# Reordering the split products of a packed matrix step: plain halves, whole products, special halves

## The chip, the cores and the metric

The kernel runs on one core of one Trainium2 chip. The metric is the device time of one execution in microseconds (us). Before the change it is 2581.51 us, the median of three runs that lie between 2581.0 and 2581.97 us.

TensorE is the matrix engine; the profile shows it as two rows, PE for the matmuls and PEld for the loads of the stationary operand (the weights). DVE, ACT and POOL are the vector, scalar and GpSimd engines, SP is the queue that issues most of the DMAs.

## What is computed

The reference filters a sequence in the frequency domain and sends the result through a small network:

```python
X = np.fft.rfft(x, axis=1)              # x: (8, 3008, 256)
Y = X * (filt_r + 1j * filt_i)[None]
y = np.fft.irfft(Y, n=3008, axis=1)
h = y.reshape(8 * 3008, 256) @ w_in     # (256, 2048)
out = (h - np.tanh(h)) @ w_out          # (2048, 256)
```

Everything is float32.

## The kernel before

The length 3008 is taken as 64 times 47. A transform over the 64 (`first`) is followed by a *middle stage* (`middle`): a transform over the 47, the product with the filter, and the transform back over the 47. A last transform over the 64 (`last`) gives the tokens, and the network follows: `up` (by `w_in`), `shrink` (h minus tanh h) and `down` (by `w_out`).

The eight batch elements are cut into 48 groups, and each group into four units of the network. The network keeps TensorE busy all the time; the transforms of later batch elements are spread between its units. A loop over the units (line 1280) calls `up`, and at fixed places in it the callback `t(k)` (line 1325) takes one step of whatever stage is due: `first`, `last`, or a step of `middle`. Everything is issued in program order, written out by hand; no planner moves an instruction. So the order of the Python calls is the order on each engine.

`middle(b)` runs for seven batch elements (b = 1 to 7; element 0 goes another way). It goes over four slices `o = 0..3`. Each slice has

- a *forward* step (lines 433 to 443): `packed` writes four PSUM banks (`t`, `o3`, `o1`, `o2`) from the tile `a2`. ACT copies banks 2 and 3 (line 438), DVE adds and subtracts (lines 440 and 441);
- the product with the filter, on DVE (lines 445 to 461);
- a *backward* step (lines 462 to 469): `packed` writes four banks (`o0`, `t`, `y`, `o1`) from the tile `xy`; ACT and DVE copy them out (line 465), and DMAs take them to memory.

The bank names other than `t` are shared with the network: `o0` to `o3` are the accumulators of `down`, `y` is a bank of `up`. After a forward step TensorE goes on with `down` (line 747), after a backward step with `down` or `up` (lines 747 and 577).

`packed` (line 346) makes 16 small products at once. Each product has 24 rows by 32 columns of weights and sits in its own square of the 128 by 128 array: row strip `q` (0 to 3, partitions 32q up) and column strip `col` (0 to 3). Row strip q writes bank q; column strip col writes the partitions 32 col and up of that bank. A *whole* product streams 512 columns of data: two blocks of 256 that use the same weights.

In the last slice, `o = 3`, one block of four of the products is special and needs other weights. These four products are *split*: a *plain half* (256 columns, usual weights) and a *special half* (256 columns, other weights), both in the same square of the array, the second writing the other half of the bank's columns. In the forward step these are the four products of column strip 3, one in each row strip. In the backward step they are the four products of row strip 3. So a split step has 12 whole products, 4 plain halves and 4 special halves, 20 in all; a *plain* step (o = 0, 1, 2) has 16 whole products.

A float32 product is carried out in two passes over the data: the profile shows two weight loads and two matmuls for every product. A split step thus has 40 matmul records, a plain step 32.

Before the change the plain half stands at its place in the order of q and col (in the forward step the 4th, 8th, 12th and 16th product, in the backward step the 13th to 16th), and the four special halves come behind all of them.

Of the kernel before, what the change touches and what calls it, by code (L numbers as in the profile page):

```python
# [17 lines left out]
BATCH, SEQ, DM = 8, 3008, 256  # L18
# [93 lines left out]
def kernel(  # L112
# [9 lines left out]
    nc = tc.nc  # L122
# [97 lines left out]
    def sums(u):  # L220

        w = (wu if u < 4 else wd)[:, :, 256 * (u % 4):256 * (u % 4) + 256]
        V.tensor_add(w[:, 4], w[:, 6], w[:, 3])
        yield
        for to, one_in, less in ((5, 4, 0), (2, 1, 5), (6, 0, 6)):
            V.tensor_sub(w[:, to], w[:, one_in], w[:, less])  # L226
            yield

    def begun(tiles, job, queue=nc.sync):
        j = converted(tiles, *job, queue)  # L230
        next(j)
        return j
# [3 lines left out]
    def weights(tiles, jobs, queue, began, ahead, after=()):  # L236

        began += [begun(tiles, job, queue) for job in jobs[len(began):ahead]]
        yield
        for k in range(len(jobs)):  # L240
            pending[0] = len(jobs) - k
            for n, _ in enumerate(began[k]):
                yield
                if after and n == 2 and k + 1 < len(jobs):
                    next(began[k + 1])
            if k + ahead < len(jobs):
                began.append(begun(tiles, jobs[k + ahead], queue))
            pending[0] = len(jobs) - k - 1
            for u in dict(after).get(k, ()):
                yield from sums(u)  # L250
# [94 lines left out]

    def packed(banks, o, weight, data):

        late = []
        for q, bank in enumerate(banks):
            part = slice(PAD * q, PAD * q + NH)  # L350
            for col in range(4):
                to, at = bank[PAD * col:PAD * col + PAD], data(q, col)[part]
                plain, special = (wide[part, weight(q, col, last)] for last in (0, 1))
                if o == 3 and 3 == (col if weight is WAYS[0] else q):
                    late.append((to[:, 1], special, at[:, DM:2 * DM]))
                    to, at = to[:, 0], at[:, 0:DM]
                else:
                    to = to.rearrange("p n c -> p (n c)")
                nc.tensor.matmul(to, plain, at, start=True, stop=True)  # L359
        for to, special, at in late:  # L360
            nc.tensor.matmul(to, special, at, start=True, stop=True)  # L361

    def forth(g, at, z):

# [62 lines left out]
    def middle(b, z):  # L427
# [4 lines left out]
        for o in range(4):  # L432
            there = z(("t", "o3", "o1", "o2"))
            packed(there, o, WAYS[0],
                   lambda q, col: a2[:, 2 * col:2 * col + 2].rearrange("p n c -> p (n c)"))
            there = [bank.rearrange("p n c -> p (n c)") for bank in there]
# [24 lines left out]
            yield  # L461
            again = z(("o0", "t", "y", "o1"))
            packed(again, o, WAYS[1], lambda q, col: xy[:, (0, 2, 1, 3)[col]])
            for j, copy in enumerate((ACT.copy, V.tensor_copy) * 2):
                copy(nn[:, 2 * j:2 * j + 2], again[j])
# [483 lines left out]
    with tc.tile_pool(name="tr", bufs=2) as tr, tc.manual_schedule():  # L949
# [16 lines left out]
        with tc.tile_pool(name="pro", bufs=1) as pro, \  # L966
# [112 lines left out]
            for c in range(3):  # L1079
# [7 lines left out]
                for k in (0, 4):  # L1087
                    nc.sync.dma_start(xt[0:64, k:k + 4], dram(x.tensor, (8 * c + k) * DM,
                                                              [[NR * DM, 64], [1, 4 * DM]]))
                    at = max(k, lo)  # L1090
# [77 lines left out]
            for g in range(last_g + 1):  # L1168
# [25 lines left out]
                if g == 2:  # L1194
                    next(turning)
                    ahead = [begun(tiles1, job, queue=G) for job in jobs[5:7]]
# [6 lines left out]
            late = weights(tiles1, jobs[5:], G, ahead, 3,  # L1203
                           after={6: (0,), 8: (1,), 10: (2, 4)})
# [5 lines left out]
        with tc.tile_pool(name="dn", bufs=2) as dn, \  # L1210
# [58 lines left out]
            for _ in range(4):  # L1269
                nc.tensor.matmul(warm[0:KM], mats[:, 3 * KM:4 * KM], mats[:, 3 * KM:3 * KM + 256],  # L1270
                                 start=True, stop=True)
# [8 lines left out]
            for U in range(total + 2):  # L1280
                i, u = divmod(U, 4)
                if U == 6:
                    assert not pending
                    late = (None for u in (3, 5, 6, 7) for _ in sums(u))
                if U == 3:
                    G.dma_start(mats[:, 0:10 * PAD], wide_d[0:KM])
                if U < total:
                    p, c = groups[i]
# [119 lines left out]
```

## Time and profile before

| what | value |
|---|---|
| time, median of three runs | 2581.51 us (2581.0 to 2581.97) |
| span of the profiled execution, first to last instruction | 2578.0 us |
| what the median has beside that span | 3.5 us; the profiled execution's own time is not listed apart from its span |
| PE busy | 2553.1 us, 99% of the span |
| DVE, ACT, POOL busy | 71%, 64%, 57% of the span |
| matmuls of `packed`, line 359 | 2 x 896 records, 33.4 us busy forward, 31.7 us backward |
| matmuls of the special halves, line 361 | 2 x 56 records, 7.2 us busy each way |

How to read it: the engines' busy times overlap, so the engine that is busy nearly all of the span and waits for nobody sets the time. Matmul records overlap one another too: a record lasts from the first column that goes in to the last result that comes out, so in a full stream a new matmul begins long before the record of the one ahead ends. What a matmul costs is therefore read from the distance between two starts, not from its duration. In the list in order of time, matmuls of one line that follow one another are merged into one row: start, length, engine, line, operation, tiles, shape, count. Starts and lengths there are in us.

### The profile page before, as it was taken

How to read it: one execution, taken by the hardware profiler on the slowest of the kernel's cores; microseconds unless marked ns; L12 is line 12 of the kernel's file. 1: busy time of each engine (PE TensorE's matmuls, PEld its weight loads, DVE VectorE, ACT ScalarE, POOL GpSimd, SP SyncE). 2: the span in 40 equal slices, each digit the busy share in tenths (PEclk: the TensorE clock that was granted, in tenths of full speed). 3: DMA queues.
4: the chain of work that ended last, by engine and by line, in shares of the span. 5: the costliest groups of instructions: out<-in, count | busy, mean ns of one | idle time of the engine just before them, and what ended most of it. 6: DMA issues, size and time to landing. Idle time of an engine off the chain costs nothing.

```text
span 2578.0 us, 43442 instructions
## 1 busy us (share of the span) xinstructions
PE 2553.1 (99%) x16596; PEld 2173.1 (84%) x16596; DVE 1818.7 (71%) x2235; ACT 1661.7 (64%) x2482; POOL 1465.8 (57%) x1124
## 2 busy tenths in 40 slices
PE   8999999999999999999999999999999999999998
PEld 7678889888898888988888888888889888898887
DVE  6888776777567775778657876588766877555555
ACT  4566666666666666666666666666666666666665
POOL 4356665666556655565646565566655766555552
PEclk9999999999999999999999999999999999999999
DMA  8863225332333324343243332334231322110110
GB/s 223 278 176 102 64 48 124 99 98 59 82 82 97 99 48 90 85 102 82 58 95 89 92 85 52 87 97 112 64 72 35 93 65 49 28 32 18 25 22 18
DMA packets 345334, 214.30 MB, mean 83 GB/s; under 512 B 245338, under 2 KB 316536, under 8 KB 341470
## 3 DMA queue, kind: packets, MB, share of 16 engines
q1 hardware_dynamic: 321551, 170.82, 28.1%
q10 hardware_dynamic: 12142, 23.60, 2.9%
q0 software_dynamic: 11424, 17.03, 2.4%
q8 instruction: 132, 2.16, 0.4%
q14 instruction: 85, 0.69, 0.1%
HBM read 130.72 MB, written 83.39 MB: 83 GB/s over the span
## 4 chain that ended last, share of the span: by engine, by line
PE 94%; DVE 2%; DMA 2%; ACT 1%; issue 1%; POOL 0%; ACTq 0%; SPq 0%; POOLq 0%; DVEq 0%
PE o L747 43%; PE x L577 25%; PE z L577 12%; PE y L577 6%; PE pm L359 2%; PE pu L536 2%; PE pf L306 1%; DMA ct<-a 1%; DMA x<-in_x_dram 0%; DMA ct<-e 0%; PE pm L361 0%; PE pf L294 0%; DVE h L699 0%; PE o L802 0%; DVE wd L226 0%
## 5 line engine op out<-in xcount | busy, mean ns | idle before, releaser
L747 PE MATMUL o<-t,wd 128*128 128x256 f32 (+1 forms) x3008 | 762.1, 376 | 0.0
L557 POOL TENSOR_TENSOR t<-h 128x512 f32<-128x512 f32 (+1 forms) x186 | 305.8, 1644 | 733.6 <-DVE h L699 713.7
L699 DVE TENSOR_TENSOR h<-h,y 128x1024 f32<-128x1024 f32 (+1 forms) x384 | 573.5, 1493 | 166.5 <-ACT y L695 163.0
L747 PEld LDWEIGHTS o<-t,wd 128*128 128x128 f32 x3008 | 569.2, 190 | 82.4 <-POOL o L775 15.1
L577 PE MATMUL x<-tu,wu 128*128 128x256 f32 (+1 forms) x2256 | 579.0, 379 | 0.0
L747 PE MATMUL o<-h,wd 128*128 128x256 f32 (+1 forms) x2256 | 572.8, 376 | 1.7 <-DVE h L699 1.7
L583 ACT COPY s<-x 128x512 f32<-128x512 f32 (+1 forms) x188 | 108.8, 579 | 595.8 <-PE x L577 554.1
L747 PEld LDWEIGHTS o<-h,wd 128*128 128x128 f32 x2256 | 426.0, 190 | 71.4 <-issue 20.5
L577 PEld LDWEIGHTS x<-tu,wu 128*128 128x128 f32 x2256 | 420.9, 190 | 66.8 <-issue 13.5
L692 ACT ACTIVATE y<-y 128x1024 f32<-128x1024 f32 (+1 forms) x384 | 399.2, 1040 | 12.1
L695 ACT ACTIVATE y<-y 128x1024 f32<-128x1024 f32 (+1 forms) x384 | 399.8, 1041 | 4.6
L689 ACT ACTIVATE y<-h 128x1024 f32<-128x1024 f32 (+1 forms) x384 | 400.3, 1043 | 3.5 <-DVE h L625 1.7
L558 POOL TENSOR_TENSOR t<-h,t 128x512 f32<-128x512 f32 (+1 forms) x186 | 305.4, 1642 | 14.6
L560 POOL TENSOR_TENSOR t<-h,t 128x512 f32<-128x512 f32 (+1 forms) x186 | 288.2, 1549 | 0.0
L559 POOL TENSOR_TENSOR t<-h 128x512 f32<-128x512 f32 (+1 forms) x186 | 287.5, 1546 | 0.0
L583 ACT COPY u<-x 128x512 f32<-128x512 f32 (+1 forms) x376 | 213.7, 568 | 56.3 <-PE x L577 53.6
L625 DVE COPY h<-x 128x512 f32<-128x512 f32 (+1 forms) x188 | 127.9, 680 | 135.0 <-PE x L577 134.7
L577 PE MATMUL y<-ut,wu 128*128 128x256 f32 (+1 forms) x752 | 190.1, 375 | 0.6 <-ACT a L296 0.6
L577 PE MATMUL x<-ut,wu 128*128 128x256 f32 (+1 forms) x752 | 190.1, 375 | 0.6 <-DVE h L625 0.6
L577 PE MATMUL z<-ut,wu 128*128 128x256 f32 (+1 forms) x752 | 190.2, 375 | 0.4 <-DVE h L617 0.4
L577 PE MATMUL z<-tu,wu 128*128 128x256 f32 (+1 forms) x752 | 190.1, 375 | 0.4 <-DVE h L633 0.4
L600 DVE TENSOR_TENSOR h<-y,s 128x512 f32<-128x512 f32 (+1 forms) x188 | 126.6, 673 | 68.5 <-PE y L577 61.9
(194 smaller groups left out, 2743.1 us busy)
## 6 DMA issues: line engine op xcount, KB each, us to landing
ft<-filt SPq DMA_DIRECT2D x28, 1024.0 KB
ct<-nn SPq DMA_DIRECT2D x56, 512.0 KB
e<-ct SPq DMA_DIRECT2D x47, 512.0 KB
a<-ct SPq DMA_DIRECT2D x112, 192.0 KB
out_dram<-ot SPq DMA_DIRECT2D x1248, 16.0 KB
x_sb<-in_x_dram SPq DMA_DIRECT2D x74, 256.0 KB
ct<-a ACTq DMA_DIRECT2D x62, 256.0 KB
gt<-g_pairs SPq DMA_DIRECT2D x42, 128.0 KB
```

Of the source, the lines that this page charges most:

```text
L557: by.tensor_sub(t[0], b[0][1], b[0][0])
L558: by.tensor_sub(t[1], b[1][1], t[0])
L559: by.tensor_sub(t[2], b[1][1], b[0][1])
L560: by.tensor_sub(t[3], b[1][0], t[1])
L577: nc.tensor.matmul(bank[:, k], wu[:, q - 1, (2 * u + k) * 128:(2 * u + k + 1) * 128], rhs[q - 1], start=(first and k == 0), stop=True, ski ...
L583: ACT.copy(t, X)
L625: V.tensor_copy(h[:, 2, :, 0:w], X)
L689: ACT.activation(y[k], ht[k], AF.Arctan, scale=TURN)
L692: ACT.activation(y[k], y[k], AF.Tanh, scale=BEND)
L695: ACT.activation(y[k], y[k], AF.Square, scale=SCALE, accum_out=y_sums[:, 2 * U + k // 2:2 * U + k // 2 + 1])
L699: V.tensor_mul(ht[k], ht[k], y[k])
L747: nc.tensor.matmul(product(q), wd[:, q - 1, (2 * u + k) * 128: (2 * u + k + 1) * 128], rhs[q - 1][:, k], start=(u == 0 and k == 0 and q == ...
```

## The change

In a split step `packed` collects its products in three lists and issues first the four plain halves, then the twelve whole products, then the four special halves. Plain steps issue the same 16 products in the same order as before. No product, weight or operand is changed, and the orders on DVE, ACT, POOL and SP are the same, instruction for instruction; only TensorE's order is another in the 14 split steps (7 forward, 7 backward). The new text is one line shorter, so that line 747 of before is line 746 after, and all matmuls of `packed` stand in line 360.

```diff
     def packed(banks, o, weight, data):
 
-        late = []
+        ahead, whole, late = [], [], []
         for q, bank in enumerate(banks):
             part = slice(PAD * q, PAD * q + NH)
             for col in range(4):
                 to, at = bank[PAD * col:PAD * col + PAD], data(q, col)[part]
                 plain, special = (wide[part, weight(q, col, last)] for last in (0, 1))
                 if o == 3 and 3 == (col if weight is WAYS[0] else q):
+                    ahead.append((to[:, 0], plain, at[:, 0:DM]))
                     late.append((to[:, 1], special, at[:, DM:2 * DM]))
-                    to, at = to[:, 0], at[:, 0:DM]
                 else:
-                    to = to.rearrange("p n c -> p (n c)")
-                nc.tensor.matmul(to, plain, at, start=True, stop=True)
-        for to, special, at in late:
-            nc.tensor.matmul(to, special, at, start=True, stop=True)
+                    whole.append((to.rearrange("p n c -> p (n c)"), plain, at))
+        for to, weights_of, at in ahead + whole + late:
+            nc.tensor.matmul(to, weights_of, at, start=True, stop=True)
```

On TensorE's list of instructions a forward split step turns from four times (three whole, one plain half), then four special halves into 4 plain halves, 12 whole, 4 special halves. The waits move with it: before, each row strip's first product waits for its bank and its rows of data, so that the waits stand at the 1st, 5th, 9th and 13th product. After, the four plain halves touch all four banks, and these waits stand at the 1st to 4th product. In six of the seven forward split steps (not in that of b = 1) the wait of the third row strip, bank `o1`, is among others for TensorE's own earlier matmuls; before it stands at the 9th product, after at the 3rd. In the backward step the wait for TensorE stays with the third row strip's first whole product (bank `y`), which is the 9th product before and the 13th after.

## The prediction

> **What bounds the kernel now.** I read the page first (busy time, clock, chain), then the waits of TensorE, then the list in order of time around the split steps.
>
> ```profile
> span 2578.0 us, 43442 instructions
> ...
> PE 2553.1 (99%) x16596; PEld 2173.1 (84%) x16596; DVE 1818.7 (71%) x2235; ACT 1661.7 (64%) x2482; POOL 1465.8 (57%) x1124
> ...
> PEclk9999999999999999999999999999999999999999
> ...
> PE 94%; DVE 2%; DMA 2%; ACT 1%; issue 1%; POOL 0%; ACTq 0%; SPq 0%; POOLq 0%; DVEq 0%
> ```
> ```profile
> PE pe L1049 <- POOL nn L397: 5.8, 3, 4.0
> PE o L747 <- DVE h L699: 1.7, 2, 1.6
> ```
>
> TensorE is the bound: it is busy 99% of the span at full clock and carries 94% of the chain that ended last. The two longest of its waits on other engines are 5.8 and 1.7 us in all, the first of them in the opening stage (line 1049), where no split step lies. So a microsecond taken off TensorE's stream between two middle steps should come off the time.
>
> The steps themselves: a plain backward and a split backward step, a plain forward and a split forward one, each with the matmul behind it.
>
> ```profile
> 2130.98 1.14 PE L359 MATMUL pm<-xy,mats_sb 24*32 24x512 f32 x32
> 2132.05 0.70 PE L747 MATMUL o<-t,wd 128*128 128x256 f32 x2
> ```
> ```profile
> 2183.74 1.11 PE L359 MATMUL pm<-xy,mats_sb 24*32 24x512 f32 x32
> 2184.37 1.08 PE L361 MATMUL pm<-xy,mats_sb 24*32 24x256 f32 x8
> 2185.39 0.48 PE L747 MATMUL o<-t,wd 128*128 128x256 f32 x1
> ```
> ```profile
> 2083.45 1.22 PE L359 MATMUL pm<-a,mats_sb 24*32 24x512 f32 x32
> 2084.60 0.70 PE L747 MATMUL o<-h,wd 128*128 128x256 f32 x2
> ```
> ```profile
> 2135.70 1.21 PE L359 MATMUL pm<-a,mats_sb 24*32 24x512 f32 x32
> 2136.34 1.08 PE L361 MATMUL pm<-a,mats_sb 24*32 24x256 f32 x8
> 2137.36 0.48 PE L747 MATMUL o<-h,wd 128*128 128x256 f32 x1
> ```
>
> From the first product to the next stage's first matmul a plain backward step takes 2132.05 - 2130.98 = 1.07 us, a plain forward step 1.15, a split step 1.65 in both directions. Both kinds stream the same number of columns through each square, so the split costs 0.58 us backward and 0.50 forward. All 14 are alike: the windows below show the first and the last of 14, each with 40 matmuls, and the mean.
>
> ```profile
> 327.90:329.60 1.70, 1.67 (x40) 0.60 (x40) 0.00 (x0) 0.00 (x0) 1.00 0.97 242
> ...
> 2183.70:2185.40 1.70, 1.66 (x40) 0.60 (x40) 0.44 (x1) 0.54 (x2) 1.00 0.00 0
> sum 23.80, PE 23.56 PEld 8.53 DVE 3.42 ACT 4.08; mean PE 1.68 PEld 0.61 DVE 0.24 ACT 0.29
> ```
>
> **Where the 0.58 us go.** Inside the backward step, by narrow stretches of the list (a merged row starts at its first record), and the durations in ns (least/median/most):
>
> ```profile
> 2184.06 0.79 PE L359 MATMUL pm<-xy,mats_sb 24*32 24x256 f32 x16
> 2184.19 0.66 PE L359 MATMUL pm<-xy,mats_sb 24*32 24x512 f32 x12
> 2184.80 0.41 PE L361 MATMUL pm<-xy,mats_sb 24*32 24x256 f32 x2
> 2185.05 0.41 PE L361 MATMUL pm<-xy,mats_sb 24*32 24x256 f32 x3
> ```
> ```profile
> L359 PE MATMUL pm<-xy,mats_sb x22: 374/612/612, 2183.7 to 2184.2; 24*32 24x512 f32 x14, 24*32 24x256 f32 x8
> L359 PE MATMUL pm<-xy,mats_sb x12: 587/587/587, 2184.2 to 2184.3; 24*32 24x512 f32 x12
> L361 PE MATMUL pm<-xy,mats_sb x8: 371/374/396, 2184.4 to 2185.1; 24*32 24x256 f32 x8
> ```
> ```profile
> 2184.81 0.17 PEld L361 LDWEIGHTS pm<-xy,mats_sb 24*32 24x32 f32 x6 [0.33 <-issue]
> ```
>
> The second passes of the plain halves start at 2184.06, those of the whole products at 2184.19, which is 0.45 us behind the first pass of the first product. A first pass of 256 columns, its weight load with it, holds its square 0.24 us (2184.81 to 2185.05); for a second, whose weights lie ready, I estimate 0.22 from that, so the squares of the halves are free from about 2184.28. Yet only one pass of a special half starts near there, at 2184.37; its second starts at 2184.80, and the other three special halves only then, their second passes at 2185.05. These times match the ends of the first product: its first pass ends at 2183.74 + 0.61 = 2184.35, its second at 2184.19 + 0.59 = 2184.78, and 0.02 us behind each comes a pass of the first special half. Forward it is the same, with the halves elsewhere in the order:
>
> ```profile
> 2136.16 0.76 PE L359 MATMUL pm<-a,mats_sb 24*32 24x512 f32 x12
> 2136.77 0.37 PE L361 MATMUL pm<-a,mats_sb 24*32 24x256 f32 x1
> ```
>
> 2135.70 + 0.61 = 2136.31 against 2136.34, and 2136.16 + 0.59 = 2136.75 against 2136.77. I read: the 17th product enters, pass by pass, only as the 1st completes; a later one waits behind it in order. TensorE holds 16 products at a time. The Trainium skill, "TensorE: Matmul & The Clock Gate", in its opening table, gives TensorE's queue a depth of 64; at two loads and two matmuls a product that is 16 products. By that page the place in the queue counts, not the kind of product ahead, and the time would be that of the sum below; without it the traces leave this open, which is rival two.
>
> **The change part by part.** Removed and added: nothing; 40 passes before and after, the other engines' orders untouched. Moved: the first product becomes a plain half. Times from here run from a step's first product.
>
> *Backward, seven steps.* Plain half 1: first pass 0, second pass 0.24 (the special halves show 2184.81 to 2185.05), its square free at 0.24 + 0.22 = 0.46. It completes at 0.40 and 0.24 + 0.37 = 0.61. Whole products start within 0.1 behind the halves and their second passes end as in a plain step, which then leaves at 1.07. Special half 1: first pass at 0.46 (square), second at 0.68 (square; the queue lets it in at 0.61 + 0.03 = 0.64). Special halves 2 to 4 come in order behind that entry: 0.65, 0.67, 0.68, spaced as in 2184.80 and its followers; the last one's second pass starts at 0.68 + 0.24 = 0.92. From that start to the next matmul it takes 0.30 now (2185.05 + 0.41 - 0.37 = 2185.09 to 2185.39). So the step ends at 1.22, 0.43 less than 1.65.
>
> *Forward, b = 1, one step.* Nothing waits inside; the same 1.22.
>
> *Forward, six steps.* Their third bank waits for TensorE's own earlier matmuls. The plain forward step shows the price: 1.15 against 1.07, so its 9th product starts 0.08 late, at 0.05 + 0.08 = 0.13. That wait now stands at the 3rd product: half 3 starts at 0.13, its second pass at 0.13 + 0.22 = 0.35, complete at 0.35 + 0.37 = 0.72, so that special half 4, behind the entry of special half 3's second pass, comes in at 0.75, with its second pass at 0.99 and the end at 1.29 or 1.30. All 12 whole products now stand behind this wait, not 8: they would leave at about 1.19, which is covered. Saved 1.65 - 1.30 = 0.35.
>
> *Cover and followers.* Nothing may take the gain back behind the step:
>
> ```profile
> 2137.45 1.07 ACT L438 COPY xy<-pm 128x512 f32<-128x512 f32 x2 [1.91 <-PE pm L361]
> ...
> 2183.49 0.73 POOL L775 TENSOR_TENSOR o<-pu,o 128x256 f32<-128x256 f32 x1 [1.97 <-DVE pu L773]
> ...
> 2184.86 1.07 ACT L465 COPY nn<-pm 128x512 f32<-128x512 f32 x2 [1.98 <-PE pm L359]
> ```
>
> ACT stands idle ahead of the copies, 1.91 us forward and 1.98 us backward; forward, they start some 0.4 us earlier, and the four DVE operations (lines 440 and 441) with them. Backward bank 0 is written 0.03 us later, four starts behind the halves, and ACT's first copy moves by that; were ACT's idle time gone, this would be what it costs. POOL was idle 1.97 us before 2183.49, so `t`, which line 747 reads behind the step, is long done; and plain steps reach the same followers at 1.07 with no wait. SP and POOL queues see no change; the output DMAs follow the copies.
>
> Sum: 8 x 0.43 + 6 x 0.35 = 3.4 + 2.1 = 5.5 us. The profiled span would become 2578.0 - 5.5 = 2572.5; the median stands 3.5 us above the span, so the time is 2581.5 - 5.5 = **2576.0 us**, -0.21%. Bounds of the unknown entry: at best split steps become plain ones (rival one, 7.4 us), at worst nothing is gained and the earlier wait is paid (rival two, -1 us). I take 5.5 because four coincidences to 0.03 us, in two directions, speak for completion in order. Its own range is 2575.2 to 2576.8, from 0.05 us a step either way.
>
> **The rivals.** *One: only a special half's own square holds it.* Then specials run at 0.46 to 0.5 and 0.7 to 0.75, and the whole products set the end: 1.07, or 1.19 with the wait. 8 x 0.58 + 6 x 0.46 = 7.4 us, 2574.1 us. For it: in the plain stream second passes do overtake (2184.06 ahead of 2184.19). Against: before, squares free at 2184.28 stood empty until 2184.80. The Trainium skill, "TensorEngine Tiling (Array Packing)", Tiling Modes, says tiles operate independently; by that rule this rival would hold, and the empty squares disagree.
>
> *Two: the special halves wait for the first whole product, or the gain is lost behind the step; the change does not do what it says.* Then they enter 0.03 later than now (four starts, of 16 in 0.1 us), and six steps wait 0.08 to 0.13 more: 14 x 0.03 + 6 x 0.1 = 1 us slower, 2582.5. For it: in all 14 steps the first product is whole, so the trace cannot part the two readings. Against: nothing there tells why a whole product should matter.
>
> *Three, in part:* the later special halves come in more slowly than 2184.80 and its followers, only as the first's second pass has run a while. At 0.1 to 0.2 us a step that leaves 5.5 - 14 x 0.1 = 4.1 or 2.7 us: about 2578.
>
> *Four, slower: products of one strip run one after another when they stand side by side.* The halves share a column strip forward and a row strip backward. Then the fourth half starts 3 x 0.43 = 1.3 us late and the whole products leave at 2.4: 14 x 0.72 = 10 us, 2591.6. It decides from the point at which whole products are held by 0.58 us (1.65 - 1.07). Against: the special halves of one strip start within 0.04 us of one another (2185.05, three in 0.41). The Trainium skill, "TensorE: Matmul & The Clock Gate", Part 3, lets a load overlap a running matmul only where the row group differs; that would bring it on in the seven backward steps, 2586.5 us, but 32 loads of four strips went out there beside running matmuls, so the trace disagrees:
>
> ```profile
> 2183.73 0.23 PEld L359 LDWEIGHTS pm<-xy,mats_sb 24*32 24x32 f32 x32 [0.33 <-DVE pu L773]
> ```
>
> **How the numbers follow.** Chances: the forecast 0.54, rival one 0.23, three 0.11, two 0.08, four 0.04. The range 2573.6 to 2579.0 takes in the forecast, rival one and three. A gain of 0.2% is 5.2 us; that is about what a measurement of this kernel can tell from no change. The forecast's 5.5 clears it three times in four, rival one always: faster 0.41 + 0.23 + 0.01 = 0.65; slower by over 0.2% is rival four and a little of two, 0.05; the rest, 0.30, lies within.
>
> **What would show it.** In the changed profile every split backward step should take 1.22 us to line 746 or 577, six forward steps 1.30 and that of b = 1 1.22; special half 1 should start near 0.46, its fellows near 0.65 to 0.68. Steps of 1.07 speak for rival one, special halves at 0.67 and 1.1 for rival two, halves 0.2 us or more apart for four. If the steps shorten but the span does not, the loss is in a wait behind them, and my reading of TensorE as the only bound was wrong.

## The result and the profile after

On one chip, eight runs of each kernel: the changed kernel takes 2576.27 us (median; 2573.58 to 2577.84), the kernel before 2581.27 us. The medians lie 5.0 us (0.19%) apart; the ratio of all runs is 0.9977 with a 95% interval of 0.9969 to 0.9986, that is 0.23% faster. Nine more runs of the changed kernel on another occasion gave 2574.72 against 2582.08 us, ratio 0.9975 (0.9965 to 0.9984).

The page of the changed kernel's profile (rows of parts 1, 2 and 4):

```profile
span 2576.0 us, 43442 instructions
...
PE 2548.8 (99%) x16596; PEld 2173.3 (84%) x16596; DVE 1823.4 (71%) x2235; ACT 1662.0 (65%) x2482; POOL 1464.2 (57%) x1124
...
PEclk9999999999999999999999999999999999999999
...
PE 94%; DMA 2%; DVE 2%; ACT 1%; issue 0%; POOL 0%; SPq 0%; POOLq 0%; ACTq 0%; DVEq 0%
```

TensorE is the bound as before, at the same clock. Its busy time fell by 4.3 us. The last two split steps, forward and backward, in the list in order of time (all 40 matmuls of a step are one row now):

```profile
2134.83 1.29 PE L360 MATMUL pm<-a,mats_sb 24*32 24x256 f32 x40
2136.06 0.48 PE L746 MATMUL o<-h,wd 128*128 128x256 f32 x1
```
```profile
2182.44 1.29 PE L360 MATMUL pm<-xy,mats_sb 24*32 24x256 f32 x40
2183.66 0.48 PE L746 MATMUL o<-t,wd 128*128 128x256 f32 x1
```

Both take 1.22 us to the next stage's first matmul, against 1.65 before. All 14 do. Where the first of them starts is shown here, in the kernel before and in the changed one:

```profile
327.94 1.13 PE L359 MATMUL pm<-a,mats_sb 24*32 24x512 f32 x32
```
```profile
332.18 1.29 PE L360 MATMUL pm<-a,mats_sb 24*32 24x256 f32 x40
333.40 0.92 PE L746 MATMUL o<-h,wd 128*128 128x256 f32 x3
```

From the start of the first split step to the start of the last it is 2183.74 - 327.94 = 1855.80 us before and 2182.44 - 332.18 = 1850.26 us after. The difference, 5.54 us, is 13 x 0.43; with the last step, 5.97 us were taken out, and nothing between them gave any of it back. But the first split step itself starts 4.2 us later in this profiled execution, though the two programs are the same up to there. That is why the two spans differ by only 2.0 us; the experiments come back to it.

Inside the backward step, in narrow stretches of the same list: special half 1's first pass (the row starts with it, the rest are passes behind it), the last six weight loads, and the last three second passes:

```profile
2182.89 0.69 PE L360 MATMUL pm<-xy,mats_sb 24*32 24x256 f32 x17
2183.08 0.17 PEld L360 LDWEIGHTS pm<-xy,mats_sb 24*32 24x32 f32 x6
2183.32 0.41 PE L360 MATMUL pm<-xy,mats_sb 24*32 24x256 f32 x3
```

Special half 1 starts at 0.45 us, the loads of special halves 2 to 4 begin at 0.64, and the last second pass starts at 0.88 + 0.41 - 0.37 = 0.92. Forward, the copy behind the step starts 2136.17 - 2134.83 = 1.34 us after the step's start, where it took 2137.45 - 2135.70 = 1.75 before:

```profile
2136.17 1.07 ACT L437 COPY xy<-pm 128x512 f32<-128x512 f32 x2 [1.51 <-PE pm L360]
```

### The profile page after: what moved, and what is told of

Its sections match the earlier page's. It is cut to its first block, busy times and chain, and to the rows that moved or that the text cites. A ratio compares the mean times of both kernels' runs of the same rounds, so it can differ in the third digit from the quotient of the medians.

```text
span 2576.0 us, 43442 instructions
## 1 busy us (share of the span) xinstructions
PE 2548.8 (99%) x16596; PEld 2173.3 (84%) x16596; DVE 1823.4 (71%) x2235; ACT 1662.0 (65%) x2482; POOL 1464.2 (57%) x1124
## 4 chain that ended last, share of the span: by engine, by line
PE 94%; DMA 2%; DVE 2%; ACT 1%; issue 0%; POOL 0%; SPq 0%; POOLq 0%; ACTq 0%; DVEq 0%
PE o L746 43%; PE x L576 25%; PE z L576 12%; PE y L576 6%; PE pm L360 2%; PE pu L535 2%; PE pf L306 1%; DMA ct<-a 1%; DMA x<-in_x_dram 0%; DMA filt<-in_filt_r_dram 0%; DMA ct<-e 0%; PE o L801 0%; PE pf L294 0%; DVE h L698 0%; DVE wd L226 0%
```

## Experiments

All kernels but the last are the changed kernel with a few lines of `packed` edited; the last is the changed kernel itself. Theory A is the prediction's: TensorE holds 16 products, and the (16+k)th enters, pass by pass, only as the kth completes, in order. The rivals give a special half another reason to wait. The times of `three_ahead`, `two_ahead`, `one_whole_first` and `special_13th` stand against 2581.39 us of the kernel before on the same chip, those of the other four against 2582.08. The intervals of the ratios are 4 to 6 us wide, so the times part the theories only roughly; the lengths of the steps in the traces decide.

### Three plain halves ahead

```diff
-        for to, weights_of, at in ahead + whole + late:
+        for to, weights_of, at in ahead[:3] + whole + ahead[3:] + late:
```

> Only three plain halves stand ahead of the whole products, the fourth behind them (16th). Theory A (TensorE holds 16 products, and product 16+k enters pass by pass only as product k completes, in order): the 4th special half is tied to the 4th product, now a whole one, whose second pass completes at 0.02 + 0.45 + 0.59 = 1.06; so the special half's second pass starts at 1.09 and the step takes 1.39 us instead of 1.22 (before: 1.65). Over 14 steps 0.26 x 14 = 3.6 us less than before. Rival B (each plain half that is issued early gives its own quarter of the 0.43 us): 1.33 us, 4.5 us less than before. Rival C (a special half is held only by its own square): 1.22 or less, 6 us less than before.

Measured: 2578.16 us, ratio 0.9986 (0.9976 to 0.9996), 3.2 us less than before. The last backward split step, and the last pass in it:

```profile
2181.82 1.46 PE L360 MATMUL pm<-xy,mats_sb 24*32 24x256 f32 x40
...
2182.91 0.37 PE L360 MATMUL pm<-xy,mats_sb 24*32 24x256 f32 x1
2183.21 0.48 PE L746 MATMUL o<-t,wd 128*128 128x256 f32 x1
```

The step takes 1.39 us, and a single second pass stands apart at 2182.91 - 2181.82 = 1.09. Theory A named both numbers, and 3.6 us for the time; a quarter of the gain for each half would have been 1.33.

### Two plain halves ahead

```diff
-        for to, weights_of, at in ahead + whole + late:
+        for to, weights_of, at in ahead[:2] + whole + ahead[2:] + late:
```

> Only two plain halves ahead, the other two behind the whole products. Theory A (16 products held, completion in order): the 3rd special half's second pass is tied to the 3rd product, a whole one, complete at 1.05; the 4th special half enters behind that at 1.09, its second pass at 1.33, and the step takes 1.63 us, so hardly 0.3 us in all are left of the gain over before (1.65 a step). Rival B (a quarter of the gain for each half): 1.44 us, 3.0 us less than before. Rival C (own square only): 1.22 or less, 6 us less than before.

Measured: 2582.19 us, ratio 1.0001 (0.9991 to 1.001), no difference from before. The last backward split step, with its last loads and passes:

```profile
2186.62 1.70 PE L360 MATMUL pm<-xy,mats_sb 24*32 24x256 f32 x40
...
2188.25 0.48 PE L746 MATMUL o<-t,wd 128*128 128x256 f32 x1
```
```profile
2187.26 0.15 PEld L360 LDWEIGHTS pm<-xy,mats_sb 24*32 24x32 f32 x4
2187.70 0.13 PEld L360 LDWEIGHTS pm<-xy,mats_sb 24*32 24x32 f32 x2 [0.29 <-issue]
```

The step takes 1.63 us. Two halves ahead let special halves 2 and 3 load their weights at 0.64; the loads of the 4th come only at 2187.70 - 2186.62 = 1.08, as the third product's second pass ends. Half of the halves moved, and 0.02 of 0.43 us gained: the gain does not add up half by half.

### One whole product in front

```diff
-        for to, weights_of, at in ahead + whole + late:
+        for to, weights_of, at in whole[:1] + ahead + whole[1:] + late:
```

> As the changed kernel, with one of the twelve whole products ahead of the four plain halves. Theory A (16 products held, completion in order): everything hangs on the first product; special half 1 enters with its first pass at 0.64, its second at 1.07, the others behind it, and the step takes 1.65 us as before the change: all of the gain is gone, 0 +- 0.5 us against before. Rival B (plain halves early give the gain): 1.23 us, 5.9 us less than before. Rival C (own square only): the same 1.23 or less.

Measured: 2580.58 us, ratio 1.0 (0.9991 to 1.001), no difference from before.

```profile
2188.02 1.72 PE L360 MATMUL pm<-xy,mats_sb 24*32 24x512 f32 x40
2189.67 0.48 PE L746 MATMUL o<-t,wd 128*128 128x256 f32 x1
```
```profile
2188.66 0.10 PEld L360 LDWEIGHTS pm<-xy,mats_sb 24*32 24x32 f32 x1 [0.29 <-issue]
2189.09 0.17 PEld L360 LDWEIGHTS pm<-xy,mats_sb 24*32 24x32 f32 x6 [0.33 <-issue]
```

1.65 us. The plain halves still run early, in the 2nd to 5th place, yet the second load of special half 1 comes at 0.64 and the other loads at 1.07, to 0.01 us as in the kernel before (2184.37 and 2184.81 in a step from 2183.74). What the first product is decides, so a special half is not held by its own square, nor by the plain halves as such.

### Special halves in the 13th to 16th place

```diff
-        for to, weights_of, at in ahead + whole + late:
+        for to, weights_of, at in ahead + whole[:8] + late + whole[8:]:
```

> Plain halves, 8 whole products, special halves (13th to 16th), 4 whole products (17th to 20th). Theory A (16 products held): the special halves need no entry and run at 0.46 and 0.67, but now whole products are late: the last enters at 0.68, second pass at 1.14, step 1.65 us, no gain over before (0 +- 0.5 us). Rival C (own square only): the special halves are done by 0.9 and the whole products end the step at 1.1 to 1.2 us, 6 to 7.5 us less than before.

Measured: 2581.87 us, ratio 1.0002 (0.9992 to 1.0011), no difference from before.

```profile
2187.28 1.72 PE L360 MATMUL pm<-xy,mats_sb 24*32 24x256 f32 x40
...
2188.39 0.62 PE L360 MATMUL pm<-xy,mats_sb 24*32 24x512 f32 x3
2188.94 0.48 PE L746 MATMUL o<-t,wd 128*128 128x256 f32 x1
```

1.65 us again. The special halves run early, their first passes from 0.46 us and their second from 0.67; the step is now ended by three 512-column passes of whole products that start only at 1.11 us. The delay belongs to the 17th to 20th place and falls on whatever stands there. This parts theory A from a rule about whole or special products, which the trace of before could not.

### No split at all

```diff
-                if o == 3 and 3 == (col if weight is WAYS[0] else q):
+                if o == 4 and 3 == (col if weight is WAYS[0] else q):
```

> Leaves out the special halves' own weights: the slice o = 3 is run as 16 whole products with the usual weights, so the special columns are wrong. The same columns are streamed with 16 products. Theory A (16 products held): backward steps 1.07 us, forward 1.15 (1.07 for b = 1), that is 7.6 us less than before and 1.7 us less than the changed kernel: this is all that the 17th to 20th product still cost. If a split cost came from the columns and not from the number of products, these steps would stay at 1.22.

Measured: 2574.05 us, ratio 0.997 (0.9959 to 0.9981).

```profile
2180.96 1.14 PE L360 MATMUL pm<-xy,mats_sb 24*32 24x512 f32 x32
2182.03 0.48 PE L746 MATMUL o<-t,wd 128*128 128x256 f32 x1
```

The same columns in 16 products take 1.07 us. So of the 0.58 us that the split cost backward, the new order recovers 0.43; 0.15 us a step stay, what the 17th to 20th product still cost. Forward, six of the seven steps take 1.15 us and that of b = 1 1.07, as forecast. The 1.7 us that this leaves between this kernel and the changed one are seen in the steps alone: the medians on the same chip, 2574.05 and 2574.72, can't be told apart.

### The forward direction alone

```diff
-        for to, weights_of, at in ahead + whole + late:
+        for to, weights_of, at in (ahead + whole if weight is WAYS[0] else whole + ahead) + late:
```

> Plain halves first only in the seven forward split steps; backward steps in the order of before. If the two directions add up: forward 1.22 us, backward 1.65, 7 x 0.427 = 3.0 us less than before, and each forward step shifts what comes behind it by 0.43 us, the backward ones by nothing. If the forward gain were given back by a wait behind the step, the shift would be less than 0.43.

Measured: 2578.17 us, ratio 0.9987 (0.9978 to 0.9997), 3.9 us less than before. Forward split steps take 1.22 us, the backward ones 1.65:

```profile
2134.83 1.29 PE L360 MATMUL pm<-a,mats_sb 24*32 24x256 f32 x40
2136.05 0.48 PE L746 MATMUL o<-h,wd 128*128 128x256 f32 x1
...
2182.43 1.72 PE L360 MATMUL pm<-xy,mats_sb 24*32 24x512 f32 x40
2184.08 0.48 PE L746 MATMUL o<-t,wd 128*128 128x256 f32 x1
```

Set side by side with the trace of before, matmul by matmul, this trace steps forward by 0.42 or 0.43 us at each forward split step and stays level everywhere else behind the first of them. The two directions add up.

### The banks' waits at the head of every forward step

This one adds to the changed kernel:

```diff
+        if weight is WAYS[0]:
+            n = len(whole) // 4
+            whole = [whole[n * q + col] for col in range(n) for q in range(4)]
         for to, weights_of, at in ahead + whole + late:
```

> The changed kernel, and in the forward steps the whole products go round the row strips (first column strip of all four row strips, then the second ...), so that the four banks' waits stand at the first four products also in plain steps. Theory W1 (the 0.08 us in the plain forward step are a wait met in mid-stream, which costs nothing when it stands at the head, since TensorE reads ahead while the stage before still runs): the 13 plain forward steps of 1.15 us become 1.07, 1.0 us less than the changed kernel, 7.0 us less than before. Theory W2 (bank o1 has to wait for TensorE's earlier matmuls to end, wherever the wait stands): they stay at 1.15 or become 1.17. Split steps 1.22 in both.

Measured: 2574.77 us, ratio 0.9974 (0.9964 to 0.9983). A plain forward step (o = 2 of b = 7) with its weight loads:

```profile
2080.54 1.14 PE L363 MATMUL pm<-a,mats_sb 24*32 24x512 f32 x32
2081.61 1.99 PE L749 MATMUL o<-h,wd 128*128 128x256 f32 x8
```
```profile
2080.53 0.23 PEld L363 LDWEIGHTS pm<-a,mats_sb 24*32 24x32 f32 x32 [0.33 <-DVE h L635]
```

The same step of the kernel before has its loads spread over 0.31 us:

```profile
2083.45 0.31 PEld L359 LDWEIGHTS pm<-a,mats_sb 24*32 24x32 f32 x32 [0.33 <-DVE h L633]
```

1.07 instead of 1.15 us, and so in all 13 plain forward steps that took 1.15. The first product still starts 0.31 us behind the start of the matmul ahead of it, so the 0.08 us have not moved to the front of the step. W1 holds, and the traces show what the 0.08 us are. TensorE has an instruction of its own for one of the waits (EVENT_SEMAPHORE, carried out by its sequencer, which the profile names PEldq). In the step of the kernel before, and in that of this kernel:

```profile
L359 PEldq EVENT_SEMAPHORE  x1: 51/51/51, 2083.5 to 2083.5; - x1
```
```profile
L363 PEldq EVENT_SEMAPHORE  x1: 51/51/51, 2079.8 to 2079.8; - x1
```

In the kernel before it runs 0.02 us behind the step's first load; the 9th product's first load then starts at 0.10 us, against 0.05 in a forward step of 1.07, and the products behind it are 0.07 to 0.08 late. In this kernel it runs 0.69 us ahead of the first load, while `up` is still on the array. The kernel before has one inside each of its 13 plain forward steps of 1.15 us and none inside the 8 of 1.07. All of its 65 in line 359 take 51 ns, and those inside the steps start 0.020 to 0.022 us behind the first product each time. So it is a fixed price of the instruction's place among the products, and not a bank that comes free late.

The 13 steps save 13 x 0.08 = 1.0 us against the changed kernel, but 0.3 of it is given back behind them. Bank `o1` is now filled by the 15th product instead of the 12th, so ACT's copies behind a plain forward step start at 1.36 us instead of 1.31, and in each of b = 2 to 7 one later matmul of `up`, which starts in both as a copy of ACT ends, comes 0.05 us later. Here a forward step and that matmul, in the changed kernel and in this one (5.76 and 5.82 us apart):

```profile
433.81 1.14 PE L360 MATMUL pm<-a,mats_sb 24*32 24x512 f32 x32
...
439.57 1.02 PE L576 MATMUL x<-tu,wu 128*128 128x224 f32 x4
```
```profile
432.33 1.14 PE L363 MATMUL pm<-a,mats_sb 24*32 24x512 f32 x32
...
438.15 1.02 PE L579 MATMUL x<-tu,wu 128*128 128x224 f32 x4
```

So 0.7 us are left in the trace; the time (2574.77) can't be told from that of the changed kernel on the same chip (2574.72).

### More runs of the changed kernel

> The changed kernel once more, with more runs. The 14 split steps save 14 x 0.427 = 6.0 us between the first and the last of them. Theory O1 (the opening stage, ahead of the first split step, varies from execution to execution and is not touched by the change): over more runs the median moves towards 6 us less than before, and the first split step starts anywhere in the 327.9 to 332.2 us that the profiles so far show. Theory O2 (the change makes the opening stage about 1 us longer): the median stays at 5 us less than before and the first split step again starts at 332.

Measured: 2574.72 us, ratio 0.9975 (0.9965 to 0.9984), 7.4 us less than before. The 6.0 us of the split steps (0.9977) lie within both intervals. The first split step of this profiled execution, and the second longest of TensorE's waits in it:

```profile
334.04 1.29 PE L360 MATMUL pm<-a,mats_sb 24*32 24x256 f32 x40
335.26 0.92 PE L746 MATMUL o<-h,wd 128*128 128x256 f32 x3
```
```profile
PE pa L370 <- DMA a<-a: 2.4, 1, 2.4
```

It starts at 334.0, later than the 327.9 to 332.2 that O1 named. This execution took 2579.32 us, the longest of the nine, while their median is 4.6 us less. Over the profiled executions of all these kernels the first split step starts between 327.9 and 334.0 us. Here one wait of 2.4 us for a DMA in the opening stage does part of it; the changed kernel's first profile has another set of waits there. So the opening varies by several us from execution to execution, O1. That the change moves the opening by less than a microsecond or so is not excluded: there is one profile of the kernel before, and it has the earliest start of all.

## Why the prediction was right

- *TensorE is the bound, and what is saved comes off the time.* Right: 13 x 0.43 us between the first and the last split step, with no wait behind.
- *The 17th product enters as the 1st completes; 16 products are held.* Right, and shown by four orders that differ in nothing but place: 1.39, 1.63, 1.65 and 1.65 us, each forecast to 0.01 us. The Trainium skill, "TensorE: Matmul & The Clock Gate", opening table, gives a queue depth of 64; with two loads and two matmuls a product the runs agree with it. What is counted, 16 products, 32 matmuls or 64 loads and matmuls together, they don't part, since every matmul here has a load of its own (16596 of each on the page). Loads may come in earlier than the rule in its plain words has it: in the last backward split step of the kernel before, special half 1's first load starts at 0.32 us, before any matmul of the first product has ended.
- *Backward 1.22 us; special half 1 at 0.46, the others from 0.65, the last second pass at 0.92.* Right: 1.22, 0.45, 0.64, 0.92.
- *Forward with the wait of the third bank, 1.30 us.* Wrong: 1.22 in all seven. The step that failed is "half 3 starts at 0.13": I took the 0.08 us of the plain forward step for a wait for the bank and carried them over to the wait's new place. They are the price of the 51 ns semaphore instruction among the products. In the last forward split step of the changed kernel it runs 0.69 us ahead of the first load and costs nothing, and half 3 starts at 0.01; `strips_in_turn` shows the same for plain steps. The term of the six forward steps was 2.1 us and measured 6 x 0.43 = 2.6, so the sum should have been 6.0, not 5.5.
- *The median stands 3.5 us above the span, the span becomes 2572.5.* Wrong as a fixed distance: the changed kernel's profiled execution took 2577.84 us at a span of 2576.0, 1.8 us apart. The profiled execution of before had an early opening, so that its span lay low against the median. That 2576.0 came so near 2576.27 is luck: the sum was 0.5 us short, and the medians lay 5.0 us apart on this occasion and 7.4 on the other.
- *Rivals.* One (own square): refuted by `one_whole_first`; its time for a step, 1.07, appears only with 16 products. The Trainium skill, "TensorEngine Tiling (Array Packing)", Tiling Modes, has the tiles operate independently; that holds among the 16 products held, and not for the 17th. Two (bound to whole products): refuted by the changed kernel, whose special halves come in at 0.45 and 0.65 and not at 0.67 and 1.1, and by `special_13th`, where whole products themselves are late. Three (later special halves slower to come in): not seen, three in 0.04 us. Four (strips in series): not seen, the halves of one strip ran side by side.

With 6.0 us in place of 5.5 the chance of 0.65 for a gain beyond 0.2% (5.2 us) would have been higher. The two measurements, 0.23% (0.14 to 0.31) and 0.25% (0.16 to 0.35), do not settle by themselves whether 0.2% is passed; the 6.0 us are read from the steps.

## What to carry to other kernels

Where many small products are in flight in different squares of the array, count them against what TensorE holds: here 16 float32 products. If there are more, those that complete soonest belong at the very front and short ones at the very end; one long product in first place undoes the whole gain. Waits that cost TensorE an instruction of their own belong at the head of such a burst rather than in the middle; look also at what the new order makes later, as ACT's copies showed. A gain of a few microseconds is read from the steps in the trace, since the opening stage alone varies by as much.

## What was not expected of the hardware

The gain is a staircase, not a slope: with 4, 3 and 2 plain halves in front a step takes 1.22, 1.39 and 1.63 us, since each late product is tied to one early product. And in 13 plain steps 0.08 us hung on the place of one semaphore instruction of 51 ns (1.15 to 1.07 us). Within the products held, passes overtake one another: special half 1's first pass (2182.89) starts ahead of whole products' second passes, which were issued long before it; the Trainium skill, "TensorE: Matmul & The Clock Gate", Part 3, has matmuls start and end strictly in program order, and for the starts this trace disagrees. The recorded ends are out of that order too (0.83 us for this pass, 1.07 for the first of the others), though the profile models the ends of matmuls; what goes in order is the letting in of the 17th and later products.
